# Experts in pairs of token tiles, with a seven-product block scheme on two thirds of the first matrix product

## The chip, the cores and the metric

The kernel runs on one core of one Trainium2 chip. The metric is the device time of one execution in microseconds (us), lower is better. A core has five engines that run side by side and meet at semaphores: TensorE (PE, matrix products; PEld is its weight load), VectorE (DVE), ScalarE (ACT), GpSimd (POOL) and SyncE (SP, which here issues all DMAs). TensorE reads SBUF and writes PSUM, which has eight banks of 128 x 512 float32; GpSimd and the DMAs do not reach PSUM.

## The reference

Three layers follow one another: a recurrent attention, a dense layer with a mish-like gate, and eight experts that are all computed for all tokens and added with weights P. Only the last is changed:

```python
def _moe2_ref(x, w_gate, w1, w2):          # x: 3072 x 384, w1: 8 x 384 x 1024, w2: 8 x 1024 x 384
    logits = x @ w_gate
    P = np.exp(logits - logits.max())
    for _ in range(8):
        P /= P.sum(1, keepdims=True) + 1e-09
        P /= P.sum(0, keepdims=True) + 1e-09
        P *= N / E
    out = np.zeros((N, D))
    for e in range(E):
        h = np.maximum(x @ w1[e], 0.0)
        out += P[:, e:e + 1] * (h @ w2[e])
    return out
```

## The kernel before

Everything is transposed: a tile of 512 tokens is `xT[n]`, three chunks (k = 0, 1, 2) of 128 features by 512 tokens. There are six such tiles (NT = 6). The hidden width of an expert, 1024, is cut into eight blocks f of 128 (NF2 = 8).

Precision comes from splitting. Each operand is held as a rounded high part and a remainder, and each product of a 128 x 128 weight block with a 128 x 512 block of x is three matmuls (`PASSES`: high by high, high by low, low by high). ScalarE writes the high part, GpSimd or VectorE subtracts to get the low part.

A unit is one (expert e, tile n, block f); there are 8 x 6 x 8 = 384, in the order e, n, f. A unit has 9 matmuls of the first product (`first`, line 254: three chunks of x, three passes, into one of four rotating banks `h`), then `relu` (line 322 on ScalarE writes the high part of g from PSUM, line 323 on VectorE the low part), then 9 matmuls of the second product (`second_e`, line 371: three output chunks, three passes, into banks `y0` to `y3`). The loop at line 912 issues, for each i, `first(i+1)`, `second_e(i-2)`, `relu(i)`, so that a unit's first product is two units ahead of its second. Engines run their instructions in the order in which the program writes them.

Once per tile and expert (f = 7) the sums are weighed: VectorE multiplies the bank by P (line 384), GpSimd adds it to `acc[n]` (line 385). In the last expert VectorE also transposes the result (line 388) and four DMAs per chunk write it out. The last tile of the last expert has its own form: `second_t` (line 412) has 12 matmuls of 384 columns a unit and yields tokens by features, so that no transpose is due at the end; the sum so far is turned by TensorE through `turn` (line 401).

Weights are loaded and split once per expert and block (`load_e`, `split_e`, lines 209 to 221); x is split for every tile and expert anew (`split_x`, lines 195 and 196).

Before the experts stands the dense layer: 96 units i of the same shape (NM = 96), with a long chain on ScalarE, VectorE and GpSimd (`mish_e` to `mish_lo`) between first and second product. `mish_hi` (line 312) and `mish_lo` (line 317, GpSimd) write g; `second_m` (line 334) of unit i - 3 is issued after `first(i+1)`. In the last units of that layer the first expert units' first products are already issued (`first(i+1)` with i + 1 >= 96), which fills TensorE while the last gates are computed.

Of the kernel before, what the change touches and what calls it, by code (L numbers as in the profile page):

```python
# [27 lines left out]
DM = H * D  # L28
# [7 lines left out]
E = 8  # L36
# [15 lines left out]
CB = 13  # L52
NCA = 12
# [17 lines left out]
def layers(ctx: ExitStack, tc: tile.TileContext, a, out, bad, general):  # L71
# [105 lines left out]
    mst = ExitStack()  # L177
    AE = (pool, pool)
# [20 lines left out]
    w1, w2 = {}, {}  # L199
    epieces = [(e, f, w) for e in range(E) for f in range(NF2) for w in (0, 1)]  # L200
    NEP = len(epieces)
    eraw, epos = {}, [0, 0]

    def load_e(upto):
        while epos[0] < min(upto, NEP):
            m = epos[0]
            e, f, w = epieces[m]
            eraw[m] = mr.tile([128, DM], F32, name=f"er{m}", tag="vq"[w])
            nc.sync.dma_start(eraw[m], a[("w1", "w2")[w]][e, f])
            epos[0] += 1  # L210

    def split_e(upto, eng=pool):
        while epos[1] < min(upto, NEP):
            m = epos[1]
            load_e(m + 1)
            e, f, w = epieces[m]
            t = wA.tile([128, 2, KI, 128], F32R, name=f"we{m}", tag="w")
            th, tl = (t[:, k].rearrange("p k f -> p (k f)") for k in range(2))
            raw = eraw.pop(m)
            act.activation(th, raw, AF.Copy)  # L220
            eng.tensor_tensor(tl, raw, th.bitcast(F32), op=ALU.subtract)  # L221
            (w1, w2)[w][e, f] = t
            epos[1] += 1

# [6 lines left out]
    units += [(e, n, f) for e in range(E) for n in range(NT) for f in range(NF2)]  # L231
    NU = len(units)
# [13 lines left out]
    def first(i):  # L246
        e, n, f = units[i]
        w = wi[f] if e < 0 else w1[e, f]
# [70 lines left out]
    def relu(i):  # L319
        ph = U.pop(i)[0]  # L320
        g = gpl.tile([128, 2, TT], F32R, name=f"g{i}", tag="g")
        act.activation(g[:, 0], ph, AF.Relu)  # L322
        dve.scalar_tensor_tensor(g[:, 1], ph, 0.0, g[:, 0].bitcast(F32), op0=ALU.max, op1=ALU.subtract)  # L323
        gs[i] = g

# [14 lines left out]
    def evac_m(j):  # L340
        _, n, f = units[j]
        if n < NT - 1 and f == NF1 // 2 - 1:
            half[n] = hf.tile([128, KI, TT], F32, name=f"half{n}")
# [13 lines left out]
    ycnt = [0]  # L357
    TOKJ = (E - 1, NT - 1)

    def second_e(j):  # L360
        e, n, f = units[j]
        if (e, n) == TOKJ:
            return second_t(j)
        if f == 0:

            sums[n] = [bank([128, TT], f"ye{e}_{n}_{k}", f"y{(ycnt[0] + k) % 4}") for k in range(KI)]
            ycnt[0] += KI
        g = gs.pop(j)
        for k in range(KI):
            for m, (pw, px) in enumerate(PASSES):  # L370
                pe.matmul(sums[n][k], w2[e, f][:, pw, k, :], g[:, px, :],  # L371
                          start=(f == 0 and m == 0), stop=(f == NF2 - 1 and m == 2))
        if f == NF2 - 1:
            if e > 0:
                tt = sk.tile([128, 2, TT], F32, name=f"t{e}_{n}", tag="g")
            for k in range(KI):
                yo, o = sums[n][k], acc[n][:, k, :]
                if e == 0:
                    act.activation(o, yo, AF.Copy)
                    continue  # L380
                if e == 1:
                    pool.tensor_tensor(o, o, pb[0, n], op=ALU.mult)
                t = tt[:, k % 2, :]
                dve.tensor_tensor(t, yo, pb[e, n], op=ALU.mult)  # L384
                pool.tensor_tensor(o, o, t, op=ALU.add)  # L385
                if e == E - 1:

                    dve.transpose(xT[n][:, k, :], o)
                    ot = xT[n][:, k, :].rearrange("p (a b) -> p a b", b=32)
                    ov = out[n * TT:(n + 1) * TT, :].rearrange("(b i) d -> i b d", i=32)  # L390
                    for a4 in range(4):
                        c0 = k * 128 + a4 * 32
                        nc.sync.dma_start(ov[:, :, c0:c0 + 32], ot[32 * a4:32 * a4 + 32])

    accT = xT[0].rearrange("p k t -> p (k t)").rearrange("p (s d) -> p s d", s=NSUB)

    def turn(s):

        tp = bank([128, DM], f"tp{s}", "h")
        for k in range(KI):  # L400
            pe.matmul(tp[:, k * 128:(k + 1) * 128], acc[NT - 1][:, k, s * 128:(s + 1) * 128], unit,
                      start=True, stop=True)
        act.activation(accT[:, s, :], tp, AF.Copy)

    def second_t(j):
        e, n, f = units[j]
        if f == 0:
            sums[n] = [bank([128, DM], f"ye{e}_{n}_{s}", f"y{s}") for s in range(NSUB)]
        g = gs.pop(j)
# [23 lines left out]
    def load_p(e, n):  # L433
        if (e, n) == TOKJ:
            return
# [595 lines left out]
```

## Time and profile before

| | |
|---|---|
| time, median of 3 runs | 2163.51 us (2162.35 to 2164.61) |
| the profiled execution's own time | 2163.54 us |
| its span, first to last instruction | 2161.7 us |
| TensorE busy | 2108.2 us, 98% of the span, 9874 matmuls |
| VectorE, ScalarE, GpSimd busy | 42%, 42%, 38% |
| first expert matmul | starts 559.34 us into the span |

The span is read from left to right: attention, the dense layer (to about 575 us), the experts (the rest). Busy shares over the whole span mix these; a stretch of its own is read for each.

### The profile page before, as it was taken

The numbers are of one execution on the slowest core, as the hardware profiler recorded it, in microseconds if no ns is written. First come the engines' busy times: TensorE is split into PE (matmuls) and PEld (weight loads), VectorE is DVE, ScalarE is ACT, GpSimd is POOL, SyncE is SP. The second block draws the span as 40 slices with busy tenths as digits, with TensorE's granted clock in tenths as the row PEclk, the third lists the DMA queues.
The fourth block names the chain that finished last, engine by engine and source line by source line (L and its number), as shares of the span: only waits on it lengthen the run. The fifth ranks groups of instructions, "written<-read, shape, count | busy, mean of one in ns | idle before, by whom it ended". The sixth has DMA issues, their size and how long they took to land. (4 is left out here: it accounts for less than half of the span.)

```text
span 2161.7 us, 25851 instructions
## 1 busy us (share of the span) xinstructions
PE 2108.2 (98%) x9874; PEld 1749.2 (81%) x9874; DVE 914.4 (42%) x1481; ACT 902.2 (42%) x1875; POOL 820.5 (38%) x691
## 2 busy tenths in 40 slices
PE   7889999999999999999999999999999999999998
PEld 7777777788888888888888888888888888888877
DVE  9999999999623321222222212212212212212222
ACT  6899898899622322235432122122222222221111
POOL 5546777645411233352224224223422332332221
PEclk8999999999999999999999999999999999999999
DMA  7740111000100110023312001100200020011121
GB/s 238 199 148 23 30 30 45 15 12 19 31 8 15 30 40 19 26 83 104 107 37 64 5 13 42 35 0 16 67 5 4 24 57 5 13 32 20 21 39 31
DMA packets 96039, 94.82 MB, mean 44 GB/s; under 512 B 37216, under 2 KB 81952, under 8 KB 95904
## 3 DMA queue, kind: packets, MB, share of 16 engines
q1 hardware_dynamic: 95904, 93.07, 15.7%
q8 instruction: 79, 1.29, 0.3%
q14 instruction: 56, 0.46, 0.1%
HBM read 88.23 MB, written 4.82 MB: 43 GB/s over the span
## 5 line engine op out<-in xcount | busy, mean ns | idle before, releaser
L254 PE MATMUL ph<-xs,we 128*128 128x512 f32 x3456 | 848.0, 390 | 2.7 <-DVE g L323 2.7
L371 PE MATMUL ye<-g,we 128*128 128x512 f32 x3384 | 829.0, 389 | 3.5 <-DVE g L323 3.5
L254 PEld LDWEIGHTS ph<-xs,we 128*128 128x128 f32 x3456 | 647.5, 188 | 137.5 <-DVE g L323 2.9
L371 PEld LDWEIGHTS ye<-g,we 128*128 128x128 f32 x3384 | 635.0, 188 | 136.9 <-DVE g L323 4.8
L322 ACT ACTIVATE g<-ph 128x512 fp32r<-128x512 f32 x384 | 228.9, 598 | 1098.5 <-PE ye L371 1064.1
L323 DVE SCALAR_TENSOR_TENSOR g<-ph,g 128x512 fp32r<-128x512 f32 x384 | 260.4, 688 | 900.9 <-ACT g L322 900.7
L196 POOL TENSOR_TENSOR xs<-xT,xs 128x512 fp32r<-128x512 f32 x177 | 228.2, 1300 | 496.9 <-ACT xs L195 496.9
L385 POOL TENSOR_TENSOR acc<-acc,t 128x512 f32<-128x512 f32 x123 | 156.3, 1293 | 451.0 <-DVE t L384 448.6
L334 PE MATMUL x<-g,wm 128*128 128x512 f32 x864 | 216.5, 392 | 7.7 <-POOL g L317 7.5
L254 PE MATMUL ph<-xs,wm 128*128 128x512 f32 x864 | 212.2, 390 | 0.8 <-POOL xs L196 0.8
L334 PEld LDWEIGHTS x<-g,wm 128*128 128x128 f32 x864 | 160.6, 188 | 48.1 <-POOL g L317 14.1
L254 PEld LDWEIGHTS ph<-xs,wm 128*128 128x128 f32 x864 | 161.9, 188 | 37.2 <-POOL xs L196 1.2
L384 DVE TENSOR_TENSOR t<-ye,pb 128x512 f32<-128x512 f32 x123 | 82.2, 688 | 254.9 <-PE ye L371 226.7
L317 POOL TENSOR_TENSOR g<-y,g 128x512 fp32r<-128x512 f32 x96 | 124.3, 1295 | 134.7 <-ACT g L312 130.7
L221 POOL TENSOR_TENSOR we<-er,we 128x384 fp32r<-128x384 f32 x118 | 117.5, 1014 | 143.6 <-ACT we L220 143.4
L195 ACT ACTIVATE xs<-xT 128x512 fp32r<-128x512 f32 x177 | 105.4, 623 | 0.0
L261 ACT ACTIVATE e<-ph,lim 128x512 f32<-128x512 f32 x96 | 65.7, 684 | 35.6 <-DVE pn L276 30.5
L273 DVE TENSOR_TENSOR ph<-ph,e 128x512 f32<-128x512 f32 x96 | 66.6, 694 | 16.0 <-ACT e L263 15.8
L263 ACT ACTIVATE e<-e,lim 128x512 f32<-128x512 f32 x96 | 68.6, 714 | 0.0
L276 DVE SCALAR_TENSOR_TENSOR pn<-e,ph 128x512 f32<-128x512 f32 x96 | 65.8, 685 | 4.3 <-DVE v L124 0.2
L292 DVE SCALAR_TENSOR_TENSOR y<-sq,ph 128x512 f32<-128x512 f32 x96 | 65.2, 679 | 0.0
L220 ACT ACTIVATE we<-er 128x384 fp32r<-128x384 f32 x128 | 62.1, 517 | 6.3 <-DMA er<-in_w_dram 6.3
(132 smaller groups left out, 1421.4 us busy)
## 6 DMA issues: line engine op xcount, KB each, us to landing
er<-in_w_dram SPq DMA_DIRECT2D x128, 192.0 KB, 2.5
pb<-prow SPq DMA_DIRECT2D x47, 256.0 KB, 5.4
ld<-in_rkT_dram SPq DMA_DIRECT2D x24, 448.0 KB, 5.3
lt<-in_kr_dram SPq DMA_DIRECT2D x24, 384.0 KB, 5.7
raw<-in_w_in_dram SPq DMA_DIRECT2D x16, 384.0 KB, 3.2
raw<-in_w_out_dram SPq DMA_DIRECT2D x16, 384.0 KB, 3.1
seen<-in_w_in_dram SPq DMA_DIRECT2D x16, 384.0 KB, 3.2
seen<-in_w_out_dram SPq DMA_DIRECT2D x16, 384.0 KB, 3.1
```

Source lines behind the costliest of these rows:

```text
L195: act.activation(xs[:, 0, :], xT[n][:, k, :], AF.Copy)
L196: eng.tensor_tensor(xs[:, 1, :], xT[n][:, k, :], xs[:, 0, :].bitcast(F32), op=ALU.subtract)
L221: eng.tensor_tensor(tl, raw, th.bitcast(F32), op=ALU.subtract)
L254: pe.matmul(ph, w[:, pw, k, :], xs[:, px, :], start=(m == 0), stop=(m == 3 * KI - 1))
L263: act.activation(e, e, AF.Exp, scale=-1.0, bias=hmax)
L317: pool.tensor_tensor(gs[i][:, 1], y, gs[i][:, 0].bitcast(F32), op=ALU.subtract)
L322: act.activation(g[:, 0], ph, AF.Relu)
L323: dve.scalar_tensor_tensor(g[:, 1], ph, 0.0, g[:, 0].bitcast(F32), op0=ALU.max, op1=ALU.subtract)
L334: pe.matmul(sums[n][k], wo[f][:, pw, k, :], g[:, px, :], start=(f == f0 and m == 0), stop=(f == f1 and m == 2))
L371: pe.matmul(sums[n][k], w2[e, f][:, pw, k, :], g[:, px, :], start=(f == 0 and m == 0), stop=(f == NF2 - 1 and m == 2))
L384: dve.tensor_tensor(t, yo, pb[e, n], op=ALU.mult)
L385: pool.tensor_tensor(o, o, t, op=ALU.add)
```

## The change

The loop over experts is turned inside out and the first product is done on blocks of two by two.

- Tokens are taken in three pairs of tiles (q); for each pair all eight experts are run (e), and for each expert four groups g of two hidden blocks. That makes 3 x 8 x 4 = 96 groups; a group computes what four units did.
- In a group, chunks 0 and 1 of x (contraction), two hidden blocks and two token tiles form a 2 x 2 by 2 x 2 block product. It is done with seven block products on sums and differences of blocks (the Strassen-Winograd scheme): `A11 B11`, `S1 T1`, `S2 T2`, `S3 T3`, `A12 B21`, `S4 B22`, `A22 T4`. Chunk 2 (`A13`, `A23` with `X31`, `X32`) is multiplied plainly: four more. Eleven block products stand in place of twelve.
- The sums of weights S1 to S4 are made by GpSimd for each group (`w_sums`), the sums of tokens T1 to T4 once per pair (`x_sum`). The split tokens (nine operands, high and low) stay in SBUF for a whole pair, so that x is no longer split per expert.
- The eleven products go through two PSUM banks, `U_` and `Bk`, in eight steps s. A step ends with a pass over its bank (`c_out`): copied to SBUF by ScalarE (s = 0, 1, 2, 4) or added by VectorE to what stands there (s = 3, 5, 6, 7). Four 128 x 512 blocks come out, in SBUF; `c_hi` (ScalarE) and `c_lo` (VectorE) split them.
- The second product (`y_part`) is unchanged in size. Its matmuls for group G - 1 are woven between the steps of group G.
- The sum over experts is kept in `xT[n]` itself. Output is transposed (`turn`) at the start of the next pair, off the last expert; the last pair is turned by TensorE at the very end (`tail_turn`).
- In the last 16 units of the dense layer GpSimd prepares the first pair's operands and the first weights (`ready`), and the last four units are woven with steps 0 to 5 of the first group (`lead`) in place of `first`.
- The gate of the fifth tile and the small products of the iteration on P use a free moment of `Bk` in place of a bank of their own.

The core of the diff (added lines):

```diff
+    STEPS = ((("S1", "T1"),), (("A12", "B21"), ("A13", "X31")), (("S4", "B22"), ("A13", "X32")),
+             (("A22", "T4"), ("A23", "X31")))
+    STEPU = (("A11", "B11"), ("S2", "T2"), ("S3", "T3"), ("A23", "X32"))
+    def p1(G, s):
+        if s % 2 == 0:
+            prod(U_, G, *STEPU[s // 2], s == 0, True)
+        else:
+            st_ = STEPS[s // 2]
+            for j, (wn, xn) in enumerate(st_):
+                prod(Bk, G, wn, xn, j == 0, j == len(st_) - 1)
+    CB_ = {3: ("t0", 0, 0), 5: ("t2", 0, 1), 6: ("t5", 1, 1), 7: ("t3", 1, 0)}
+    def c_out(s):
+        if s in (0, 1, 2, 4):
+            act.activation(tt[("t0", "t5", "t2", 0, "t3")[s]], Bk if s == 1 else U_, AF.Copy)
+        else:
+            t = tt[CB_[s][0]]
+            dve.tensor_tensor(t, U_ if s == 6 else Bk, t, op=ALU.add)
+        if s == 2:
+            pool.tensor_tensor(tt["t2"], tt["t2"], tt["t5"], op=ALU.add)
+    def step(G, s):
+        if G < NGT:
+            q, e, g = groups[G]
+            p1(G, s)
+            for fn in slot.pop((G, s), ()):
+                fn()
+        if G > 0:
+            y_part(G - 1, s // 2, (2,) if s % 2 else (0, 1))
+        lo = []
+        if G + 1 < NGT and G < NGT:
+            if s == 0:
+                w_sums(G + 1, pool)
+            elif s < 4:
+                lo.append(w_hi(G + 1, s - 1))
+            elif s < 6:
+                lo.append(w2_hi(G + 1, s - 4))
+            if s in (4, 6):
+                load_w(G + 2, s // 2 - 2)
+        if G < NGT:
+            c_out(s)
+        for x in lo:
+            w_lo(*x, pool)
+        if s in (4, 6, 7):
+            c_lo(G, {4: 3, 6: 5, 7: 6}[s])
+        elif s == 0 and G > 0:
+            c_lo(G - 1, 7)
+        if s in CB_:
+            c_hi(G, s)
+        for fn in aux.pop((G, s), ()):
+            fn()
+        H = G - 1
+        if H >= 0 and groups[H][2] == NGR - 1 and s >= 5:
+            for t, k in {5: ((0, 0), (0, 1)), 6: ((0, 2),), 7: ((1, 0), (1, 1))}[s]:
+                y_out(H, t, k)
+        if s == 0 and G > 1 and groups[G - 2][2] == NGR - 1:
+            y_out(G - 2, 1, 2)
+    def lead(j):
+        for s in ((0,), (1, 2), (3, 4), (5,))[j]:
+            step(0, s)
...
+            if i >= NM - 1:
+                if i == NM - 1:
+                    U_, Bk = (bank([128, TT], nm, "h") for nm in ("U", "Bk"))
+                lead(i - NM + 1)
...
+    y_part(G, 1, range(KI))
+    for k in range(KI):
+        y_part(G, 3, (k,))
+        tail_out(1, k)
+    for k in range(KI):
+        y_part(G, 0, (k,))
+        y_part(G, 2, (k,))
+        tail_out(0, k)
+        tail_turn(1, k)
...
+    for k in range(KI - 1):
+        tail_turn(0, k)
+    for i in range(NSUB):
+        tail_copy(0, i, 0, 256, (act, dve)[i % 2])
+    tail_turn(0, KI - 1)
+    for i in range(NSUB):
+        tail_copy(0, i, 256, DM, (act, dve)[i % 2])
+        tail_dma(0, i)
```

`prod` issues the three passes of one block product; `w_hi`, `w2_hi` and `w_lo` split 128 x 384 weights; `y_out` is the weighing by P (VectorE) and the add (GpSimd); `x_split` splits one token operand; `slot` and `aux` hold what is hung on a given group and step (the gate of the fifth tile, the iteration on P, loads of P, the token operands of the next pair during nine steps from its predecessor's last group on, `turn`).

## Rows read from the trace of the kernel before

**Rows 1.** The page's busy line: microseconds, share of the span, instructions.

```profile
PE 2108.2 (98%) x9874; PEld 1749.2 (81%) x9874; DVE 914.4 (42%) x1481; ACT 902.2 (42%) x1875; POOL 820.5 (38%) x691
```

**Rows 2.** Windows: stretch, length, busy (x) of PE PEld DVE ACT POOL, clock, DMA.

```profile
1600.00:1800.00 200.00, 200.00 (x884) 165.68 (x883) 44.78 (x67) 45.33 (x84) 61.53 (x52) 1.00 0.09 24
```

**Rows 3.** The page's groups of expert matmuls: busy, mean ns, idle before.

```profile
L254 PE MATMUL ph<-xs,we 128*128 128x512 f32 x3456 | 848.0, 390 | 2.7 <-DVE g L323 2.7
L371 PE MATMUL ye<-g,we 128*128 128x512 f32 x3384 | 829.0, 389 | 3.5 <-DVE g L323 3.5
```

**Rows 4.** Timeline, one unit in steady state: start, duration, engine, line, operation.

```profile
2000.89 2.20 PE L254 MATMUL ph<-xs,we 128*128 128x512 f32 x9
...
2002.93 2.20 PE L371 MATMUL ye<-g,we 128*128 128x512 f32 x9
...
2004.97 2.20 PE L254 MATMUL ph<-xs,we 128*128 128x512 f32 x9
...
2005.17 0.60 ACT L322 ACTIVATE g<-ph 128x512 fp32r<-128x512 f32 x1 [2.44 <-PE ye L371]
```

**Rows 5.** Groups by line: busy, mean ns of one operation of each shape.

```profile
L322 ACT ACTIVATE g<-ph 128x512 fp32r<-128x512 f32 x384 | 228.9, 598 | 1098.5 <-PE ye L371 1064.1
...
L195 ACT ACTIVATE xs<-xT 128x512 fp32r<-128x512 f32 x177 | 105.4, 623 | 0.0
...
L220 ACT ACTIVATE we<-er 128x384 fp32r<-128x384 f32 x128 | 62.1, 517 | 6.3 <-DMA er<-in_w_dram 6.3
...
L384 DVE TENSOR_TENSOR t<-ye,pb 128x512 f32<-128x512 f32 x123 | 82.2, 688 | 254.9 <-PE ye L371 226.7
...
L385 POOL TENSOR_TENSOR acc<-acc,t 128x512 f32<-128x512 f32 x123 | 156.3, 1293 | 451.0 <-DVE t L384 448.6
...
L221 POOL TENSOR_TENSOR we<-er,we 128x384 fp32r<-128x384 f32 x118 | 117.5, 1014 | 143.6 <-ACT we L220 143.4
```

**Rows 6.** A VectorE group with both inputs in SBUF, GpSimd busy beside it.

```profile
L644 DVE TENSOR_TENSOR kd<-ld,Wk 112x512 f32<-112x512 f32 x24 | 25.2, 1050 | 0.0
```

**Rows 7.** Timeline of TensorE in the last expert.

```profile
2021.29 2.20 PE L254 MATMUL ph<-xs,we 128*128 128x512 f32 x9
...
2026.81 2.20 PE L254 MATMUL ph<-xs,we 128*128 128x512 f32 x9
...
2085.37 2.20 PE L254 MATMUL ph<-xs,we 128*128 128x512 f32 x9
...
2093.00 2.33 PE L254 MATMUL ph<-xs,we 128*128 128x512 f32 x9 [2.72 <-DVE g L323]
...
2097.80 2.33 PE L254 MATMUL ph<-xs,we 128*128 128x512 f32 x9
...
2123.85 2.20 PE L254 MATMUL ph<-xs,we 128*128 128x512 f32 x9
...
2132.61 2.23 PE L254 MATMUL ph<-xs,we 128*128 128x512 f32 x9
```

**Rows 8.** Timeline where the dense layer hands over to the experts.

```profile
559.09 1.29 POOL L317 TENSOR_TENSOR g<-y,g 128x512 fp32r<-128x512 f32 x1 [0.23 <-ACT g L312]
...
559.34 2.23 PE L254 MATMUL ph<-xs,we 128*128 128x512 f32 x9
...
561.41 2.20 PE L334 MATMUL x<-g,wm 128*128 128x512 f32 x9
...
562.75 1.29 POOL L317 TENSOR_TENSOR g<-y,g 128x512 fp32r<-128x512 f32 x1 [2.38 <-ACT g L312]
```

**Rows 9.** The window of the dense layer's last units, columns as in rows 2.

```profile
500.00:680.00 180.00, 179.97 (x795) 146.18 (x794) 97.02 (x174) 93.07 (x174) 58.03 (x48) 1.00 0.06 18
```

**Rows 10.** Timeline at the end.

```profile
2147.24 8.51 PE L412 MATMUL ye<-we,g 128*128 128x384 f32 x48
...
2154.22 2.19 DVE L418 SCALAR_TENSOR_TENSOR xT<-ye,Pm,xT 128x384 f32<-128x384 f32 x4 [3.36 <-PE ye L412]
...
2154.87 1.90 SPq L419 DMA_DIRECT2D out_dram<-xT  x4
```

More of the change, by code (lines that the diff above doesn't have):

```diff
@@ L355, in evac_m @@
             yield
[L357 to L409, printed above, removed]
-        for s in range(NSUB):
-            for m, (pw, px) in enumerate(PASSES):
-                pe.matmul(sums[n][s], g[:, px, s * 128:(s + 1) * 128],
-                          w2[e, f][:, pw].rearrange("p k f -> p (k f)"),
-                          start=(f == 0 and m == 0), stop=(f == NF2 - 1 and m == 2))
-        if f == NF2 - 1:
-            for s in range(NSUB):
-                o, gc = accT[:, s, :], n * NSUB + s
-                dve.scalar_tensor_tensor(o, sums[n][s], Pm[:, gc, e:e + 1], o, op0=ALU.mult, op1=ALU.add)
-                nc.sync.dma_start(out[gc * 128:(gc + 1) * 128, :], o)
@@ L463, in gate_out @@
         else:
-            both = pl.tile([32, 2, TT], F32, name=f"gt{n}", tag="g")
-            g32, gt = both[:, 0, :], both[:, 1, :]
+            g32, gt = (pl.tile([32, TT], F32, name=f"gt{n}_{j}", tag="w") for j in range(2))
             pool.memset(g32, 0.0)
@@ L531, in layers @@
         at += ln
-    for i in range(NM, NU):
-        xkey[i] = (units[i][0], units[i][1])
     last = []
@@ L839, in layers @@
+    hf = ctx.enter_context(tc.tile_pool(name="hf", bufs=NT - 1, side="right"))
+    with mst:
         nc.sync.dma_start(graw, a["w_gate"])
@@ new lines, in layers @@
+    if bad is not None:
+        G0 = E * NGR + 4
+        for m in range(2 * NF1):
+            z = G0 * 8 + 6 * m
+            at_(aux, z // 8, z % 8, lambda m=m: load_seen(m))
+            at_(aux, (z + 8) // 8, (z + 8) % 8, lambda m=m: flag(m))
+        z = G0 + 2 * NF1
+        at_(aux, z, 4, range_check)
+        at_(slot, z + 1, 2, range_bad)
+    for G in range(NGT):
+        for s in range(6 if G == 0 else 0, 8):
+            step(G, s)
+    G = NGT - 1
+    c_lo(G, 7)
+    if groups[G - 1][2] == NGR - 1:
+        y_out(G - 1, 1, 2)
@@ new lines, in layers, with tail_out, tail_turn @@
+    tb = [Y[1][2], Y[0][0], Y[0][1], U_], [U_, Bk, Y[1][0], Y[1][1]]
+    ot = [wA.tile([128, 2, DM], F32, name=f"ot{i}", tag="w") for i in range(4)]
+    def tail_out(t, k):
+        o = xT[NT - 2 + t][:, k, :]
+        t_ = tt["y", k]
+        dve.tensor_tensor(t_, Y[t][k], pb[E - 1, NT - 2 + t], op=ALU.mult)
+        dve.tensor_tensor(o, o, t_, op=ALU.add)
+    def tail_turn(t, k, subs=range(NSUB)):
+        for i in subs:
+            pe.matmul(tb[t][i][:, k * 128:(k + 1) * 128], xT[NT - 2 + t][:, k, i * 128:(i + 1) * 128], unit,
+                      start=True, stop=True, skip_group_check=True)
```

362 lines of the change are left out of this document (237 added, 125 removed).

## The prediction

> **What bounds the kernel now.** The page's busy line comes first [rows 1]: TensorE 98% of the span, no other engine above 42%. A share is a mean over stages, so the next view is a window in the middle of the experts [rows 2]: 200.0 of 200 us busy, granted clock 1.00, VectorE 45, ScalarE 45 and GpSimd 62 us of 200. A busy TensorE may still run below its pace, so the grouped rows [rows 3] and the timeline [rows 4] follow. In the groups, 6840 expert matmuls waited 6.2 us in all; in the timeline a block of nine follows the last after 2.04 us, and a unit of eighteen takes 4.08 us (2000.89 to 2004.97). So one matmul of 512 columns costs 0.2267 us, whichever product it is in, and the experts' time is that price times a count until another engine makes TensorE wait.
>
> **Fewer matmuls.** Before: 384 units x 18 = 6912. After: a group has 11 block products x 3 passes = 33, and the second product, 36 as for four units before; 96 x 69 = 6624. Removed are 288, and 288 x 0.2267 = 65.3 us if TensorE stays the bound. The operands keep their shapes, so I take the same price per matmul.
>
> **Does it stay the bound?** A group now lasts 69 x 0.2267 = 15.64 us where four units lasted 16.32. Its steps begin at 0, 2.04, 3.40, 5.44, 7.48, 9.52, 11.56 and 13.60 us. Load per group, by the prices of [rows 5]:
> - ScalarE: four copies out of PSUM and four relus at 0.60, five splits at 0.52: 7.4 us.
> - VectorE: four adds and four low parts at 0.69: 5.5 us.
> - GpSimd: five low parts at 1.01, one add at 1.29, four sums of 128 x 128. The trace has none of that size; it lies between nothing and the 1.01 of 128 x 384. From 1.01 and 1.29 a straight line gives 0.45, which I take. Together 8.2 us (6.4 to 10.4).
>
> Every fourth group adds six weighings on VectorE (4.1 us) and six adds on GpSimd (7.8). GpSimd is the fullest, 16.0 us in such a group, and in four groups 4 x 8.2 + 7.8 = 40.6 of 62.6 us. No engine is full, so what matters is the order.
>
> Each bank is alone in its role, so TensorE must wait for its reading before it writes again, where before it had four banks in turn. A reader starts 0.2 us after the matmuls' pace ends (2004.97 to 2005.17, [rows 4]). Bk of step 3 is written until 6.80; VectorE adds it from 7.00 to 7.69; the next write is at 9.52: 1.83 us to spare. For steps 5 and 7 it is 1.83 again, for step 1 1.92, for U_ 1.8 to 2.6. For g the low parts are ready several us ahead of their matmuls. The weights' chain (sums, high part, low part, all within five steps) ends near 11 us and is wanted at 15.64. After an expert's end GpSimd carries three to four us of adds into the next group; its add for step 5 then ends near 9.7, wanted at 11.08. Hence nothing in a steady group: 0, with 0.3 us per group (29 us) as the far end, since the trace has no such narrow hand-over.
>
> One input of VectorE's low part moves: it read PSUM and SBUF before and now reads SBUF twice. An operation of that kind in the attention, beside a busy GpSimd, took 1.05 us [rows 6] where 0.69 was usual [rows 5]. At 1.05 four low parts cost 1.4 us more, within the reserve. The Trainium skill ("SBUF — State Buffer", Who interferes with whom) speaks against the change here: a VectorE instruction with two SBUF inputs contends with a GpSimd instruction that reads SBUF, and the loser is blocked for the whole instruction. The row agrees in sign; it shows +0.36 us, not a whole GpSimd operation. The first rival takes the rule in full.
>
> **Where the stalls of the last expert go.** Three times a unit there takes 5.5 us (2021.29 to 2026.81), 4.4 us lost in all. One takes 7.63 (2085.37 to 2093.00): 3.55 lost. Three more carry a `turn` and take 4.80 (2093.00 to 2097.80): 2.2. One takes 8.76 (2123.85 to 2132.61): 4.7 [rows 7]. Sum 14.8 us. TensorE waits there for g's low part (line 323), and in the code's order VectorE has transposes in front of it, each of which needs an add of GpSimd first. After, the transposes stand a group later, when the adds are done, and the last pair uses TensorE. So -14.8; what replaces it is in the tail.
>
> **Hand-over from the dense layer.** The low part of unit 92 ends at 560.38 and is wanted at 561.41; that of 93 ends at 564.04 [rows 8]. After, only 3, 6, 9 and 6 matmuls stand where 9 stood, so these second products come 1.36, 0.68, 0 and 0.68 us earlier in turn, and ScalarE's copies of the new banks (0.60 each) stand ahead of the gate's steps. Unit 92's is wanted at 559.34 + 0.68 = 560.02 and waits 0.3; it runs to 562.4, and steps 1 and 2 to 563.8. For unit 93, ScalarE first waits for step 0's product (560.2), copies it (0.6) and then does the gate's six operations at some 0.6: its high part comes at 564.5, not before 562.75, the low part at 565.9: a wait of 2.2. The next two, by the same steps, wait 0.3 and 0.1, and T4, whose low part is due one step after it is issued, about 1. That makes 4 us, between 0 (an earlier GpSimd) and 10. `ready` also puts some 24 us on GpSimd (13 operations at 1.29, five at 1.01, sums of 1.8) beside the last nineteen units, some 75 us, in a stretch in which it was 32% busy [rows 9]; it fits, and splits of x that stood there go.
>
> **Changes of pair.** Twice, in nine steps, ScalarE takes nine splits more (0.62), VectorE nine low parts (0.69 to 1.05) and GpSimd four sums (1.29). VectorE's adds then come up to 2.4 us later and the 1.83 us are used up at two or three places: 1.5 us each, 3 in all, between 0 and 10. Later `turn` puts six transposes and 24 output DMAs ahead of weight loads on SP's queue; these are issued a group ahead, so I cost them at 0.
>
> **Tail.** Before, the last 48 matmuls end at 2147.24 + 8.51 = 2155.75 and the last DMA issue at 2154.87 + 1.90 = 2156.77 [rows 10]: 1.0 us. After, the last 36 matmuls have six weighings and adds (1.38 us a pair) on VectorE and two of the turns between them; a turn of three cost 0.72, so one of four 0.96. Counted from the last first product, the 39 matmuls behind it alone would take 8.8 us. VectorE can begin its six pairs once the first sum is whole (15 matmuls, 3.4 us) and ends near 12. A turn (1.0), the last copies out of PSUM (up to 0.6 each, two engines, some 2 us) and four DMA issues (1.90 in all) end it near 17: 8 us beyond, 7 more than before (4 to 11).
>
> **Sum.** 2161.7 - 65.3 - 14.8 + 0 + 4 + 3 + 7 = 2095.6 us of span. The profiled execution took 1.8 us more than its span, 2163.54 us, the median being 2163.51: so 2097 us.
>
> **Rivals.**
> 1. The steady group leaks. Against: 1.8 us to spare at each hand-over. For: single banks, and GpSimd and VectorE in each other's way. If each low part of step 5 waits for a whole add of GpSimd (1.29), the add of step 7 just keeps its time in a plain group, but after an expert's end it is 0.5 to 1 us late; with 24 such ends and small leaks elsewhere, 0.1 to 0.3 us per group, 10 to 29 us: 2107 to 2126. This is the rule of the Trainium skill cited above, taken in full; no row shows a whole block of that kind. Chance 0.18.
> 2. Slower than before. The mechanism is U_ and Bk: a reading that comes late in every group makes TensorE wait at each of the three VectorE hand-overs of Bk. The gain of 66 us is used up at 0.69 us a group, that is when VectorE's three adds come 2.06 us late each instead of 0. At 2.2 us late, 3 x 0.37 x 96 = 107 us: 2204. Against: VectorE has 5.5 us of work in 15.6. Chance 0.05.
> 3. The dense layer's end is disturbed more than I think: `ready` delays GpSimd's `mish_lo`, which had only 1.0 us to spare at unit 92, by one operation (1.29) in each of sixteen units: 20 us: 2117. Against: GpSimd's load there. Chance 0.06.
> 4. The change does less than it says, a product of the scheme being needed twice: then 0 to 65 us remain. The step tables count eleven, so 0.01.
>
> **How the numbers follow.** The forecast has 0.70. Its own range, from the low ends (0, 0, 4: 2087) to the higher ones together (10, 10, 11: 2114). To hold 8 in 10, the range leaves out rival 2 and the upper part of rival 1: 2086 to 2122. A measurement of this kernel tells about 0.2% (4.3 us) from no change. All but rival 2 and scraps are faster: faster 0.93, same 0.02, slower 0.05.
>
> **What would show each step.** TensorE's matmul groups: 6624 expert matmuls with blocks of nine still 2.04 us apart. A group of 15.6 us in the timeline; if it is longer, the wait on `U` or `Bk` and its releaser name the leak: VectorE's low part ahead of its add for rival 1, the add itself for rival 2. The wait list of TensorE around 560 to 590 us for the hand-over (`mish_lo`'s g for rival 3); about a third and two thirds through the experts, around 1060 and 1565 us, for the pairs; the last 20 us for the tail. The prediction is wrong if the window in mid-experts has TensorE below 199 of 200 us, or the matmul's price is not 0.2267.

## The result and the profile after

| | before | after |
|---|---|---|
| median, us | 2164.06 (2162.35 to 2164.77, 4 runs) | 2134.61 (2132.73 to 2136.76, 4 runs) |
| profiled execution, us | 2163.54, span 2161.7 | 2136.76, span 2134.7 |

The ratio is 0.9865, with a 95% interval of 0.9848 to 0.9882: faster by 1.35%. Forecast were 2097 us with 2086 to 2122, so the sign was right and the time lies 38 us above the forecast, outside the range. The span stands against a forecast of 2095.6, 39.1 us less.

The page's busy line of the kernel after, to be read beside [rows 1]:

```profile
PE 2072.7 (97%) x9586; PEld 1698.5 (80%) x9586; DVE 1247.0 (58%) x1891; ACT 1208.6 (57%) x2486; POOL 1353.8 (63%) x1395
```

It says little: 288 matmuls fewer, the other engines fuller, none full. The window in the middle of the experts, columns as in [rows 2]:

```profile
1600.00:1800.00 200.00, 198.31 (x864) 161.27 (x863) 93.21 (x134) 88.40 (x169) 122.88 (x140) 1.00 0.27 66
```

TensorE is busy 198.3 of 200 us: below the 199 that the prediction named as its limit. And 864 matmuls fit where 884 did. The groups by line that answer to [rows 3] and [rows 5] (busy, mean ns of one, idle before and who ended it):

```profile
L872 PE MATMUL y<-g,w 128*128 128x512 f32 x3456 | 916.0, 392 | 0.0
...
L825 PE MATMUL U<-xc_T,wc 128*128 128x512 f32 x288 | 83.3, 397 | 10.5 <-ACT tc L847 10.5
...
L763 ACT ACTIVATE wc<-er 128x384 fp32r<-128x384 f32 x192 | 99.2, 517 | 73.6 <-POOL er L779 73.6
```

The second row is the lead: TensorE's first product waits 10.5 us for a copy by ScalarE; and the third says that ScalarE, in front of a weight's high part, waits 73.6 us for GpSimd. The prediction had cost neither.

From the starts of the 96 groups in the timeline of TensorE, the 39.1 us divide so (a plain group is one from the eighth on that has none of these peculiarities):

| where | measured, us | forecast | difference |
|---|---|---|---|
| 20 groups behind an expert's end | 16.58 each, where the plain ones have 15.75 | as the plain ones | +16.6 |
| 84 groups, from the eighth on | 15.75 without that | 15.64 | +9.3 |
| one group (the 70th) with the range check's small product in `Bk` | 16.12 | as the plain ones | +0.4 |
| first group (hand-over) | 23.44 | 15.64 + 4 | +3.8 |
| second group | 19.80, of it 1.4 the last gate's six matmuls | 15.64 + 1.4 | +2.8 |
| third to seventh group | 83.55 | 5 x 15.64 | +5.4 |
| four groups at the changes of pair | 67.60 | 4 x 15.64 + 3 | +2.0 |
| start of the first expert product | 562.63 | 559.34 | +3.3 |
| everything else | | | -4.5 |

Each of the 20 groups is the second one of a new expert, in whose beginning GpSimd still adds the old expert's sums. Behind the first expert of a pair nothing is added on GpSimd (`y_out` with e = 0), and the group there, the 38th, has 15.75. Of the 3.3 us of the start, 2.2 lie ahead of unit 60 of the dense layer, where code and order are the same as before: in the first 310 us the granted clock was 0.93 in this execution and 0.96 in the one before, and in the runs below the start came between 556.99 and 564.18 in the kernels that leave the weights' place alone. The rest is the change's: units 80 to 95, in which `ready` works, took 64.7 us where they took 63.7. The last line is probably what the sum had left standing of the small waits of before; it is not traced piece by piece. The first two lines are two thirds of the miss, and the experiments begin there.

The tail came as forecast. [rows 10] are answered by the last issues of output, which end at 2128.37 (2124.04 + 4.33), 16.1 us behind the last first product at 2112.29, where the forecast said near 17; the last turns of TensorE end 1.4 us before:

```profile
2126.56 0.46 PE L1150 MATMUL U<-unit,xT 128*128 128x128 f32 x2
...
2124.04 4.33 SPq L1162 DMA_DIRECT2D out_dram<-ot  x8
```

The stalls of the last expert [rows 7] are gone: from the eighth group to the last but one, no wait of TensorE is longer than 0.54 us.

### The profile page after: what moved, and what is told of

The parts are those of the page before. It is cut to its first block, busy times and chain, and to the rows that moved or that the text cites. A ratio compares the mean times of both kernels' runs of the same rounds, so it can differ in the third digit from the quotient of the medians.

```text
span 2134.7 us, 27915 instructions
## 1 busy us (share of the span) xinstructions
PE 2072.7 (97%) x9586; PEld 1698.5 (80%) x9586; DVE 1247.0 (58%) x1891; ACT 1208.6 (57%) x2486; POOL 1353.8 (63%) x1395
## 4 chain that ended last, share of the span: by engine, by line
PE 71%; DVE 13%; POOL 6%; issue 5%; ACT 4%; DMA 0%; SPq 0%; DVEq 0%; POOLq 0%; ACTq 0%
PE y L872 31%; PE Bk L825 19%; PE U L825 11%; PE x L303 4%; PE ph L230 4%; POOL xT L889 2%; DVE q L140 1%; DVE ph L249 1%; DVE y L268 1%; DVE g L864 1%; DVE q L142 1%; DVE A L585 1%; DVE v L129 1%; DVE pn L252 1%; DVE kd L543 1%
## 5 line engine op out<-in xcount | busy, mean ns | idle before, releaser
L872 PE MATMUL y<-g,w 128*128 128x512 f32 x3456 | 916.0, 392 | 0.0
L872 PEld LDWEIGHTS y<-g,w 128*128 128x128 f32 x3456 | 647.9, 188 | 140.7 <-issue 0.2
L858 ACT ACTIVATE g<-tc 128x512 fp32r<-128x512 f32 x384 | 242.9, 633 | 638.9 <-DVE tc L850 638.8
L850 DVE TENSOR_TENSOR tc<-Bk,tc 128x512 f32<-128x512 f32 x288 | 199.1, 691 | 672.5 <-PE Bk L825 631.9
L864 DVE SCALAR_TENSOR_TENSOR g<-tc,g 128x512 fp32r<-128x512 f32 x384 | 323.6, 843 | 85.1 <-ACT g L858 77.9
L769 POOL TENSOR_TENSOR wc<-er,wc 128x384 fp32r<-128x384 f32 x192 | 198.1, 1032 | 275.7 <-ACT wc L763 275.7
L825 PE MATMUL Bk<-xc_X,wc 128*128 128x512 f32 x864 | 243.7, 390 | 0.0
L769 POOL TENSOR_TENSOR w<-er,w 128x384 fp32r<-128x384 f32 x192 | 202.0, 1069 | 59.7 <-ACT w L783 59.7
L889 POOL TENSOR_TENSOR xT<-xT,tc 128x512 f32<-128x512 f32 x120 | 171.4, 1450 | 50.0 <-DVE tc L888 50.0
L847 ACT ACTIVATE tc<-U 128x512 f32<-128x512 f32 x288 | 170.1, 590 | 33.1 <-PE U L825 25.7
L763 ACT ACTIVATE wc<-er 128x384 fp32r<-128x384 f32 x192 | 99.2, 517 | 73.6 <-POOL er L779 73.6
```

What stands on the lines that cost most here:

```text
L769: eng.tensor_tensor(flat(t[:, 1]), src, flat(t[:, 0]).bitcast(F32), op=ALU.subtract)
L825: pe.matmul(out_, w[:, pw, :], x[px], start=(start and m == 0), stop=(stop and m == 2), skip_group_check=True)
L847: act.activation(tt[("t0", "t5", "t2", 0, "t3")[s]], Bk if s == 1 else U_, AF.Copy)
L850: dve.tensor_tensor(t, U_ if s == 6 else Bk, t, op=ALU.add)
L858: act.activation(g[:, 0], tt[nm], AF.Relu)
L864: dve.scalar_tensor_tensor(g[:, 1], tt[nm], 0.0, g[:, 0].bitcast(F32), op0=ALU.max, op1=ALU.subtract)
```

## The experiments

### What makes a group long: the copy, the place, the count

In the timeline of the kernel after, around the beginning of one group behind an expert's end (it starts at 1360.75; start, duration, engine, line):

```profile
1363.05 3.02 POOL L889 TENSOR_TENSOR xT<-xT,tc 128x512 f32<-128x512 f32 x2 [1.23 <-DVE tc L888]
1366.03 0.45 POOL L776 TENSOR_TENSOR sT<-er 128x128 f32<-128x128 f32 x1
...
1367.39 0.46 POOL L779 TENSOR_TENSOR er<-er,sT 128x128 f32<-128x128 f32 x1
...
1367.88 0.53 ACT L763 ACTIVATE wc<-er 128x384 fp32r<-128x384 f32 x1 [3.41 <-POOL er L779]
1368.32 0.58 ACT L847 ACTIVATE tc<-U 128x512 f32<-128x512 f32 x1
...
1367.58 0.84 PE L872 MATMUL y<-g,w 128*128 128x512 f32 x3
1368.95 0.97 PE L825 MATMUL U<-xc_T,wc 128*128 128x512 f32 x3 [0.53 <-ACT tc L847]
```

Read from the end: TensorE waits for `U`, which ScalarE copies at 1368.32, although the product in it was written from 1364.18 to 1365.02. ScalarE stands at a weight's high part, whose source `er` GpSimd rewrites (`S4` is written in place). GpSimd does that only at 1367.39, since two late adds of y, 1.5 us each, stand ahead of the weight sums. The chain is adds, sums, high part, copy; only the last link, the order of two operations on ScalarE, is the edit of e1.

The adds are late in part because VectorE and GpSimd hold each other up. In the same trace, a little earlier:

```profile
1360.50 1.31 POOL L889 TENSOR_TENSOR xT<-xT,tc 128x512 f32<-128x512 f32 x1
1360.86 1.51 DVE L864 SCALAR_TENSOR_TENSOR g<-tc,g 128x512 fp32r<-128x512 f32 x1
...
1362.29 0.68 DVE L888 TENSOR_TENSOR tc<-y,pb 128x512 f32<-128x512 f32 x1
```

VectorE's low part, which mostly takes 0.69, begins inside an add of GpSimd and ends 0.56 us after it; the weighing behind it, which the next add waits for, is 0.82 us late by that. The second of the two late adds, begun while VectorE was at the next low part, takes 1.76 where 80 of the 120 take 1.3. That makes some 1.3 us of the chain, more than the 0.83 by which the group is longer; this is an estimate from these rows, and no run took the two engines apart. The edit of e1 leaves all this as it is and changes the order alone:

```diff
         lo = []
+        if G < NGT:
+            c_out(s)
         if G + 1 < NGT and G < NGT:
...
-        if G < NGT:
-            c_out(s)
```

> One edit on the changed kernel: in each step ScalarE's copy of the finished bank is issued before the high part of the next group's weights instead of behind it. Theory (at an expert's end the high part of er waits for GpSimd's weight sums, which stand behind three late adds of y, and the copy of U for step 2 queues behind it): the 21 groups of 16.57 us fall to the length of a plain group, 15.75, so 21 x 0.82 = 17 us less than the changed kernel's 2134.6: about 2117 us; the waits of TensorE's U on the copy (10.5 us) go. Rival (VectorE and GpSimd in each other's way, or the adds themselves late): the long groups stay, 2134 us.

Measured: 2115.76 us (ratio to before 0.9788, 0.9764 to 0.9812), 18.9 less than the kernel after. In the traces the 95 distances from one group's start to the next add up to 16.6 less. All 20 groups fell to 15.75; the one of 16.12, which the expectation had counted with them, stayed, since it waits for nothing of this chain. The same place in the timeline:

```profile
1351.04 3.02 POOL L889 TENSOR_TENSOR xT<-xT,tc 128x512 f32<-128x512 f32 x2 [1.23 <-DVE tc L888]
...
1355.39 0.46 POOL L779 TENSOR_TENSOR er<-er,sT 128x128 f32<-128x128 f32 x1
...
1353.05 0.60 ACT L847 ACTIVATE tc<-U 128x512 f32<-128x512 f32 x1 [0.35 <-PE U L825]
1355.89 0.53 ACT L763 ACTIVATE wc<-er 128x384 fp32r<-128x384 f32 x1 [2.24 <-POOL er L779]
...
1356.25 0.84 PE L825 MATMUL U<-xc_T,wc 128*128 128x512 f32 x3
```

GpSimd is as late as before and ScalarE still waits 2.24 us for it; but the copy is done, and TensorE goes on without a gap. So the late adds alone cost TensorE nothing.

The plain group kept its 15.75. The matmuls' start times in it are 0.2267 apart, but from step 6 to the next group's step 0 about 0.232. The step 6 block of six second-product matmuls, in the kernel after (1421.10 to 1422.51, 1.41 us where 6 x 0.2267 = 1.36):

```profile
1420.42 0.84 PE L825 MATMUL U<-xc_X,wc 128*128 128x512 f32 x3
1421.10 1.56 PE L872 MATMUL y<-g,w 128*128 128x512 f32 x6
1422.51 0.86 PE L825 MATMUL Bk<-xc_T,wc 128*128 128x512 f32 x3
```

They stream the g that lies in the pool `ge`. In the kernel's memory plan these two tiles start at 768 bytes modulo 1024, all other streamed tiles at 992, and the slices of the weights at 992 or 480; that is, modulo 512, at 256 against 480 for all the rest. Two edits move tiles, a third adds matmuls; all three on the kernel after:

```diff
 # e2_pad32
+    pad = sk.tile([128, 8], F32, name="pad")
+    pool.memset(pad, 0.0)
 # e3_shift: the 32 bytes of m3 fall away ahead of wA
-    lim = cp.tile([128, 2], F32, name="lim")
+    lim = cp.tile([128, 3], F32, name="lim")
...
-    m3 = cp.tile([128, 1], F32, name="m3")
+    m3 = lim[:, 2:3]
 # e4_product_twice
+            if s == 0:
+                prod(U_, G, *STEPU[0], True, True)
```

> One edit on the changed kernel: 32 unused bytes per partition ahead of the pool ge, so that its two tiles (g of the fourth quarter of a group) start at 32 modulo 64 bytes as all other operands of the matmuls do, and no longer at 0. Theory (the 0.11 us that a plain group is longer than 69 x 0.2267 comes from matmuls that read these tiles): a plain group takes 15.64 instead of 15.75 us, some 95 x 0.11 = 10 us less: about 2124 us. Rival (the slower matmuls come from what runs beside them in steps 6 to 0, whatever the address): 15.75 stays, 2134 us.

Measured: 2135.43 us (0.9862, 0.9842 to 0.9883), a plain group 15.76 to 15.77. The theory of 64 bytes fell.

> One edit on the changed kernel: a 4-byte tile is put into one that has room, so that weights, xc, er and the g of three quarters start 32 bytes lower, at 0 modulo 64, while the pool ge comes to 32 modulo 64 and xh stays at 32. If a start at 0 modulo 64 costs by itself (0.2322 instead of 0.2267 us per matmul that streams such a tile): the fourth quarter's block gets fast, and the first three quarters' 27 matmuls and the products on xc get slow, a group of 15.75 + 0.05 to 0.2 us, and the dense layer slower too: 2140 to 2160 us. If a difference between the weight's and the streamed tile's start costs: the fourth quarter stays slow, the products on xh get slow as well, the other quarters stay: 2140 to 2150. If addresses don't matter: as the changed kernel, 2134.

Measured: 2144.31 us (0.9911, 0.9894 to 0.9929), a plain group 15.86 to 15.87. The slow matmuls now ran from step 6 to the next group's step 2; from step 3 on they took 0.2267 again. Steps 0 to 2 stream `xh`, which had not moved, with weights that had. The g and xc that had moved along with the weights stayed fast. So neither 0 nor 32 is a bad start by itself: the difference to the weights is suspect.

> One edit on the changed kernel: the block product of step 0 is computed twice, the second time from the start again, so that a group has twelve block products as before the change, 36 + 36 matmuls. If TensorE's count x 0.2267 us is what the experts' time is, 288 matmuls more cost 65.3 us less what the 0.68 us longer step 0 takes out of the stall at experts' ends (up to 21 x 0.68 = 14 us): 2186 to 2200 us. If another engine or a hand-over bounds the groups, the added matmuls are partly hidden: under 2180.

Measured: 2183.07 us (1.0096, 1.0071 to 1.012), 48.5 more than the kernel after, some 3 us under the lower end of what I expected. In the trace a plain group has 16.43, 0.68 more, which is 3 x 0.2267; a group behind an expert's end 16.59 instead of 16.58, its stall swallowed by the longer step. The 95 distances between group starts add up to 49.3 us more: 95 x 0.68 = 64.6, less what the stalls took in, 20 x 0.66 = 13.2 at the experts' ends and some 2 elsewhere. The count's price holds: three matmuls cost 0.68 us in every group in which nothing else waits.

### Which places matter

The next kernels stand on e1. The first three move g's place:

```diff
 # e5_pad224 (e7_pad96: 24 for 56)
+    pad = sk.tile([128, 56], F32, name="pad")
+    pool.memset(pad, 0.0)
 # e8_swap_pools
-        g = (ge if s == 6 else gpl).tile([128, 2, TT], F32R, name=f"g{G}_{s}", tag="g")
+        g = (ge if s == 7 else gpl).tile([128, 2, TT], F32R, name=f"g{G}_{s}", tag="g")
```

> On the kernel with the copy first (2115.8 us): 224 unused bytes ahead of the pool ge, so that its tiles start where the weights and the other streamed tiles do, modulo 1024 (992). With 32 bytes they started at 800, a plain group stayed at 15.76; with the 32-byte shift of everything but xh and ge, the matmuls on xh got slow too (0.232), although xh hadn't moved. Theory (a matmul is slower where its streamed tile and its weights start at different places modulo some number between 128 and 1024 bytes): a plain group falls from 15.75 to 15.64, about 10 us: 2106 us. Rival (the steps in which these tiles are read are slow for another reason, such as what ScalarE, VectorE or GpSimd do then): 15.75 stays, 2116 us.

Measured: 2106.09 us (0.9722, 0.9697 to 0.9746), 9.7 less than e1; 83 of the 88 groups from the eighth to the last but one have 15.64, those behind an expert's end among them (the other five are the four at the changes of pair and the one with the range check), and no slow matmul is left. The same block takes 1.36 us (1419.83 to 1421.19):

```profile
1419.83 1.52 PE L872 MATMUL y<-g,w 128*128 128x512 f32 x6
1421.19 0.84 PE L825 MATMUL Bk<-xc_T,wc 128*128 128x512 f32 x3
```

The window shows how to see such a thing. TensorE is busy 200.00 of 200 us in both e1 (first) and e5 (second); the count differs, 878 and 885:

```profile
1600.00:1800.00 200.00, 200.00 (x878) 164.22 (x877) 94.47 (x135) 87.36 (x163) 124.38 (x142) 1.00 0.28 65
```

```profile
1600.00:1800.00 200.00, 200.00 (x885) 165.31 (x883) 93.04 (x133) 89.19 (x167) 127.97 (x144) 1.00 0.26 66
```

> On the kernel with the copy first: 96 unused bytes ahead of the pool ge, its tiles at 864 modulo 1024, 128 below the weights'. If the number that counts is 128: a plain group of 15.64 us. If it is 256 or more, or if addresses don't matter: 15.75 to 15.77.

Measured: one run of 2118.16 us, a plain group of 15.72 to 15.73. A difference of 128 bytes is slow as well.

> On the kernel with the copy first: the g of step 7 goes into the pool ge and the g of step 6 into the pool of the others, so that the third quarter of the second product (steps 4 and 5) streams the tiles of ge and the fourth (steps 6 and 7) no longer does. If the place of the tile sets the pace: the slow matmuls move to steps 4 and 5, those of steps 6 and 7 take 0.2267. If the time of these steps does: the slow matmuls stay in steps 6 and 7. The group 15.75 in both.

Measured: one run of 2117.77 us, 15.75 a group. The slow matmuls moved with the tile: the step 4 block now takes 1.40 us, and after the first two matmuls of step 6 the pace is 0.2267 again.

```profile
1406.85 1.56 PE L872 MATMUL y<-g,w 128*128 128x512 f32 x6
1408.25 0.85 PE L825 MATMUL Bk<-xc_B,wc 128*128 128x512 f32 x3
...
1415.12 1.52 PE L872 MATMUL y<-g,w 128*128 128x512 f32 x6
1416.48 0.84 PE L825 MATMUL Bk<-xh,wc 128*128 128x512 f32 x3
```

That leaves whether the weights are the partner, or the tile streamed before. The last run of the study tells; it stands on e10 (below), in which all streamed tiles have one place, and moves the weights alone:

```diff
-    lim = cp.tile([128, 2], F32, name="lim")
+    lim = cp.tile([128, 3], F32, name="lim")
...
-    m3 = cp.tile([128, 1], F32, name="m3")
+    m3 = lim[:, 2:3]
...
     wA = ctx.enter_context(tc.tile_pool(name="wA", bufs=NWA))
+    padw = ctx.enter_context(tc.tile_pool(name="padw", bufs=1)).tile([128, 8], F32, name="padw")
+    nc.gpsimd.memset(padw, 0.0)
```

> On the kernel of e10_early_zeros (2099.65 us): the pool of the split weights, and it alone, starts 32 bytes lower; every streamed tile stays where it was, all of them at the same place modulo 1024. Theory (what counts is where the weights start against the streamed tile): now every matmul of experts and dense layer has a difference of 32 bytes and takes about 0.232 instead of 0.2267 us: a plain group of 16.0 instead of 15.64 us, so 96 x 0.37 = 36 us in the experts and some 8 us in the dense layer: 2135 to 2146 us. Rival (what counts is a change of place between one streamed tile and the next, or the place of the tile ge by itself): nothing has changed for that, a plain group of 15.64 us, 2098 to 2104 us.

Measured: 2151.05 us (0.9934, 0.9916 to 0.9951), 51.4 more than e10, 5 us above what the theory gave. A plain group takes 16.10, that is 69 x 0.2333, and the dense layer's blocks of nine follow after 2.10 us instead of 2.04. Every matmul of experts and dense layer is slower by 2.9%:

```profile
1416.21 1.56 PE L873 MATMUL y<-g,w 128*128 128x512 f32 x6
1417.62 0.86 PE L826 MATMUL Bk<-xc_T,wc 128*128 128x512 f32 x3
```

So it is the distance between the two starts that counts: of the distances tried, modulo 512 bytes, 0 is free; the streamed tile 128, 192 or 224 bytes below the weights, or 32 above, costs. The rest of the range wasn't tried, 256 among it, so that the number may also be 256; what in the chip does it stays open.

### The hand-over, the last gate and the changes of pair

The waits of TensorE in the first group of the kernel after:

```profile
567.42 0.49 PE L303 MATMUL x<-g,wm 128*128 128x512 f32 x1 [0.52 <-ACT g L288]
568.77 2.11 PE L303 MATMUL x<-g,wm 128*128 128x512 f32 x8 [0.86 <-POOL g L293]
...
574.45 2.14 PE L303 MATMUL x<-g,wm 128*128 128x512 f32 x8 [1.30 <-POOL g L293]
577.84 0.96 PE L825 MATMUL Bk<-xc_B,wc 128*128 128x512 f32 x3 [1.25 <-DVE tc L850]
...
579.91 0.49 PE L303 MATMUL x<-g,wm 128*128 128x512 f32 x1 [0.42 <-ACT g L288]
581.32 2.14 PE L303 MATMUL x<-g,wm 128*128 128x512 f32 x8 [0.92 <-POOL g L293]
...
584.80 0.73 PE L825 MATMUL Bk<-xc_T,wc 128*128 128x512 f32 x2 [0.42 <-POOL xc_T L820]
```

On e1, the other engines' part of steps 0 to 5 goes behind the dense layer's work of the same iteration (`lead` issues TensorE's part only; the rest follows after the loop over `PO`):

```diff
-                lead(i - NM + 1)
+                lead(i - NM + 1, step_pe)
...
+            if i >= NM - 1:
+                lead(i - NM + 1, step_rest)
             if i >= NM - 16:
                 ready(i - NM + 16)
```

> On the kernel with the copy first: in the last four iterations of the dense layer the work of steps 0 to 5 on the other engines (copies out of PSUM, splits of weights, the low parts) is issued behind the dense layer's own work of the iteration and no longer ahead of it. Theory (the first group's 23.4 us, where 15.6 would do, come from the dense layer's high and low parts of g standing behind the new copies and low parts on ScalarE and GpSimd): the first group shrinks by 3 to 5 us, to 18.5 to 20.5 us: 2111 to 2113 us. Rival (they come from the dense layer's own chain of gate, e, sq and y, which now has less matmul time to hide in): within 1 us of 23.4, 2116 us.

Measured: 2116.36 us (0.9769, 0.9735 to 0.9803), no change against e1. All waits on the dense layer's g are gone, but the first group still has 22.35 us (562.06 to 584.41), and the second rose from 19.85 to 21.48. Waits of e6 in both:

```profile
575.50 0.97 PE L825 MATMUL Bk<-xc_B,wc 128*128 128x512 f32 x3 [2.84 <-DVE tc L850]
...
581.83 0.50 PE L825 MATMUL Bk<-xc_T,wc 128*128 128x512 f32 x1 [1.95 <-ACT xc_T L819]
583.17 0.72 PE L825 MATMUL Bk<-xc_T,wc 128*128 128x512 f32 x2 [0.84 <-POOL xc_T L820]
...
593.34 0.96 PE L825 MATMUL Bk<-xc_B,wc 128*128 128x512 f32 x3 [1.84 <-ACT gt L368]
```

VectorE's add of step 3 still stands behind the gate's four small adds, which now take 3.7 us where they took 1.9 in e1, and T4's splits now stand behind the next weights. The place of the miss was right, my cure moved it. Neither theory had it in full. The second group's 1.6 us are another thing, in the windows of that run (columns as in [rows 2], the granted clock third from the end):

```profile
593.00:594.80 1.80, 1.46 (x6) 1.24 (x7) 1.45 (x2) 0.70 (x2) 1.02 (x1) 0.98 0.37 109
594.80:597.40 2.60, 2.60 (x7) 1.98 (x7) 1.83 (x6) 0.63 (x1) 0.00 (x0) 0.50 0.00 0
```

After the wait of 1.84 the granted clock is 0.50, the lower of its two levels, for 2.6 us. In e1 and e5 the same wait (1.84 and 1.85) was followed by a clock of 1.00.

The next three stand on e5. Order at the hand-over, the gate's zeros, and the splits at a change of pair:

```diff
 # e9_order_handover: the step split as in e6; in the loop's end ready, then step_rest, then gate_out
-                elif x[0] == "o":
-                    gate_out(x[1], me)
             if i >= NM - 16:
                 ready(i - NM + 16)
+            if i >= NM - 1:
+                lead(i - NM + 1, step_rest)
+            for x in extra.get(i, ()):
+                if x[0] == "o":
+                    gate_out(x[1], me)
 # e10_early_zeros, on e9
-            g32, gt = (pl.tile([32, TT], F32, name=f"gt{n}_{j}", tag="w") for j in range(2))
-            pool.memset(g32, 0.0)
+            g32, gt = stage["g"]
...
+    def gate_room():
+        stage["g"] = [wA.tile([32, TT], F32, name=f"gt{j}", tag="w") for j in range(2)]
+        pool.memset(stage["g"][0], 0.0)
+
+    at_(aux, 1, 0, gate_room)
 # e11_spread_splits, on e10
-        ... (4, "B21"), (4, "T3s"), (5, "T3"), (6, "B22"), (6, "T4s"), (7, "X32"), (8, "X31"), (9, "T4")
+        ... (3, "T3s"), (5, "B21"), (5, "T4s"), (8, "T3"), (9, "X31"), (10, "B22"), (11, "X32"), (12, "T4")
```

> On the kernel with the copy first and the 224 bytes (2106.1 us): the work of steps 0 to 5 on the other engines goes behind the dense layer's own, as in the run e6_late_rest, but ahead of the gate's transpose and adds, and the splits of x, due in steps 5 and 7, go ahead of the next group's weights on GpSimd. Theory (in that run the dense layer's waits, 5 us, went, and new ones of 2.84 us behind the gate's four adds on VectorE and of 2.8 us for T4's splits came in their place, and a stall then took the granted clock down): now neither queue is in the way, the first group falls from 23.8 to 18 to 19.5 us: 2101 to 2103 us. Rival (each order only moves the stall to another consumer): 23 us or more for it, 2105 to 2107.

Measured: 2105.89 us (0.974, 0.9718 to 0.9761), which says nothing beside e5's 2106.09. In the trace the first group has 20.05 us (556.99 to 577.04) instead of 23.81, half a microsecond more than I expected. The second again has 21.41: the wait of 1.84 is followed by a clock of 0.54 from 587 to 590.

> On the kernel of e9_order_handover: the tile of the last gate is zeroed by GpSimd in step 0 of the second group instead of step 2, where the zeroing stands behind the low parts of the weights and TensorE waits 1.85 us for the gate's reading of its bank. Theory: the second group falls from 19.8 to 17.9 us, 2 us less than e9_order_handover. Rival (the reading is late anyway, since ScalarE is behind): no change.

Measured: 2099.65 us (0.9708, 0.969 to 0.9726). The second group has 17.68, 3.7 less than in e9: the wait is gone, and the fall of the clock with it. (The medians differ by 6.2; e9's executions lay between 2101.62 and 2112.14.) What is left of the hand-over, in its trace:

```profile
568.23 3.66 DVE L371 TENSOR_TENSOR lg<-gt 32x32 f32<-32x32 f32 x4
571.92 0.69 DVE L849 TENSOR_TENSOR tc<-Bk,tc 128x512 f32<-128x512 f32 x1
...
572.67 0.96 PE L824 MATMUL Bk<-xc_B,wc 128*128 128x512 f32 x3 [2.74 <-DVE tc L849]
577.84 0.94 PE L824 MATMUL Bk<-xc_T,wc 128*128 128x512 f32 x3 [0.79 <-DVE tc L849]
```

The gate's adds belong to an earlier iteration and are still ahead of step 3's add. Each of the four ends 0.04 to 0.05 us after the end of an operation of GpSimd; in e1 two do, with 0.53 and 0.96 us, and the other two, beside no such operation, take 0.18 each.

> On the kernel of e10_early_zeros: the nine splits of x at a change of pair are laid on steps in which VectorE has at most one other operation, six of them in other steps than before. Theory (the two groups of 17.54 and 16.6 us at each of the two changes come from VectorE's adds standing behind the low parts of the splits): 15.6 to 16.2 each, 4 to 6 us less than e10_early_zeros in all. Rival (GpSimd's four sums, 1.3 to 1.7 us each, hold the chain up wherever the splits stand): 17 us stays.

Measured: 2100.51 us (0.971, 0.9692 to 0.9729), no change. The two groups have 18.17 and 15.77 instead of 17.51 and 16.60: 33.94 against 34.11. The stall moved from one to the other, and the rival's 17 us each did not come either. The trace of e11 shows what holds TensorE up in the second group, and it has a part of both theories:

```profile
1070.83 1.28 POOL L798 TENSOR_TENSOR xt_T<-xT,xt_T 128x512 f32<-128x512 f32 x1
1070.85 1.81 DVE L819 TENSOR_TENSOR xc_B<-xT,xc_B 128x512 fp32r<-128x512 f32 x1 [1.22 <-ACT xc_B L818]
...
1072.58 0.68 DVE L849 TENSOR_TENSOR tc<-U,tc 128x512 f32<-128x512 f32 x1
...
1073.32 0.50 PE L824 MATMUL U<-xh,wc 128*128 128x512 f32 x1 [1.30 <-DVE tc L849]
```

The add that TensorE waits for stands behind a split's low part, and this low part ends 0.55 us after a sum of GpSimd. No run moves the sums away, so this is read and not tested.

e10 is the best of the study: 2099.65 us, 2.9% under before, in one kernel.

## Why the prediction was wrong, point by point

- **Fewer matmuls, -65.3.** Right in count and price: 6624 remained, and e4 put three matmuls per group back for 0.68 us.
- **"The same price per matmul."** This step failed. The shapes were the same, the places weren't: one of the four g tiles of a group lay at another distance from the weights. 0.11 us a group, 9.7 us between e1 and e5. The prediction looked at shapes alone, and the trace of before could not show it: there, blocks of nine came every 2.04 us in both products [rows 4].
- **"Hence nothing in a steady group."** This step failed too, and by the larger amount. It followed GpSimd's three to four us of adds behind an expert's end (in the group shown 4.1, ending 5.3 us into it), but only to the add for step 5, and took the weights' chain as done "near 11 us, wanted at 15.64". It did not ask what stands behind the weights' high part on ScalarE: the copy of `U`, wanted two steps later. That cost 20 x 0.83 = 16.6 us; in e1, which changes nothing but that order, the groups are 16.6 us shorter in sum and the median is 18.9 lower.
- **Rival 1** had the size (10 to 29 us), the place (experts' ends) and half of the mechanism. VectorE's low parts do wait for whole operations of GpSimd. The mean of the 384, 0.84 us, hides it: 246 took about 0.69, 64 took 1.40 to 1.69, and all 138 that took more than 0.72 ended 0.55 us after the end of the GpSimd operation that was running when they began. The prediction's "+0.36 us, not a whole GpSimd operation" was such a mean, too: of the 24 operations of [rows 6], 13 took some 0.68 and 11 took 1.48 or 1.49, and the one shown below this list ends 0.55 us after GpSimd's. The Trainium skill's rule ("SBUF — State Buffer", Who interferes with whom) thus holds here in full for these operations. What the rival had wrong is whom TensorE waits for: not VectorE's add, but ScalarE's copy, further down the chain. The blocked low parts are part of why the weights' sums are late, and they need not cost TensorE anything: in e5, 84 of them took 1.22 to 1.78, and the 20 groups behind an expert's end have 15.64.
- **Rival 2** needed VectorE's adds of `Bk` 2 us late in every group; in plain groups TensorE waited for none of them. Rival 3 came to 1.0 us of its 20: from 480 us to the first expert product TensorE waited twice for `mish_lo`'s g, 0.29 and 0.12, in the stretch of units 80 to 95.
- **Hand-over +4.** The mechanism was right (high and low parts of the dense layer behind the new copies), the size was not: 7.8 in the first group. The term had left out the gate's adds ahead of step 3's add on VectorE (a wait of 1.25). In the second group the gate's zeroing behind GpSimd's low parts (1.36, and 1.84 in e1) was missed altogether, and the small products in `Bk` lengthen the five groups after it, by 0.7 to 1.4 us each.
- **Stalls of the last expert, -14.8; tail, +7.** As predicted.
- **Changes of pair, +3.** 5.0.
- **The range** counted the steady group's far end, 0.3 us per group, as one unlikely case beside a high hand-over. Both came, and a cost that no term had (the place). With these two mended (e5) the kernel runs at 2106.09, still 9 us above the forecast; only the edits of the hand-over bring 2099.65. That this is 2.6 us from the forecast is in part luck: in e10 the third to seventh group and the changes of pair still cost more than forecast, and the line "everything else" makes up for it.

One of the operations of [rows 6] in the trace of before, and the GpSimd operation beside it:

```profile
11.88 1.33 POOL L650 TENSOR_TENSOR aq<-aq,lt 128x384 f32<-128x384 f32 x1
12.28 1.48 DVE L644 TENSOR_TENSOR kd<-ld,Wk 112x512 f32<-112x512 f32 x1
```

## What to carry to other kernels

When an operation is put into an in-order queue, follow not only who waits for it, but what stands behind it on its engine and when that is wanted; a wait that hurts nobody can hold a copy that TensorE needs. A window in which TensorE is 100% busy can still hide a slower pace: compare the count of matmuls, not the busy time. Before a mean duration goes into a sum, look whether it mixes two kinds: 0.84 was 0.69 and 1.5. And where a pool is added, keep streamed tiles at the same distance from the weights as before; 224 unused bytes were worth 9.7 us.

## What the runs showed of the hardware

- A float32r matmul of 512 columns took 0.2267 us where its streamed tile and its weights start at the same place modulo 512 bytes (e5), and 0.2333 at a distance of 32 (e12). The Trainium skill ("SBUF — State Buffer", Who interferes with whom) lists TensorE's two reads of SBUF, for the streamed operand and for the weights, as independent; by e12 they aren't quite, since moving the weights alone cost 2.9% of every matmul.
- A slow stretch outlasts its cause: in the kernel after about six more matmuls pass before the starts are 0.2267 apart again, so that nine matmuls on the tile of `ge` made some twenty of a group late.
- The granted clock fell to its lower level after a wait of 1.84 us in two runs (e6, e9) and not in two others (e1, e5); where it fell, the same wait cost 1.6 us more.
- A VectorE operation with both inputs in SBUF that began inside an operation of GpSimd ended a fixed time after that one's end: 0.55 us for 128x512 (138 of 138 low parts over 0.72 us in the kernel after), 0.04 to 0.05 for the gate's adds of 32x32, four of which took 3.66 us in e10 and 1.89 in e1. It went the other way too: of 120 adds of 128x512 on GpSimd, the 40 begun while VectorE was at such an operation took 1.75 us, the other 80 some 1.3, of which 76 began beside a VectorE operation with one input in PSUM.
